# Retention and gated feed-forward on one core: eight instead of ten blocks of the second token group by plain fp32, and transfers spread differently

## The chip, the cores and the metric

The kernel runs on one core of one Trainium2 chip. The metric is the device time of one execution in microseconds (us); lower is better. The median of 3 runs of the kernel before is 608.78 us (608.66 to 608.83). Five engines with queues of their own work side by side: PE multiplies matrices, DVE (VectorE), ACT (ScalarE) and POOL (GpSimd) work on elements, SP only issues transfers (DMAs), which POOL and ACT can issue too.

## The reference, cut to what matters

```python
# q, k, v: (4, 8, 768, 64); gamma: one decay per head
state = gamma * state + outer(k[t], v[t])      # for each batch and head, over 768 steps
y[t]  = scale * (q[t] @ state)
x = y as (3072 tokens, 512)                    # heads side by side
h = x @ w_in                                   # 512 x 2048
out = (h * erf(softplus(h))) @ w_out           # 2048 x 512, all to about fp32 accuracy
```

The weights come as 64-bit floats, so the kernel makes 32-bit ones of them with integer operations on DVE (lines 232 to 280).

## The kernel before, in words

**Units of work.** The sequence is cut into 24 chunks of 128 tokens (6 per batch row); two chunks are a token group of 256, so there are 12 groups, 0 to 11. A "block" (`ft`) is one of the 16 column blocks of 128 of `w_in`.

**Two ways to multiply.** Plain: `hidden_of(ft, g)` (line 691) does one block for one group with four fp32 matmuls of 256 columns; the trace shows each as two records. Split: weights and inputs are split into three fp32r parts, `hi`, `lo` and `dif` (`split_weights` line 315, `split` line 329: ACT makes `hi`, DVE `lo` and `dif`), and three products replace one fp32 product. `unit(g, n)` (line 726) does two blocks for one group: 24 matmuls of 256 columns. `pair_unit(g, ft)` (line 758) does one block for two neighbouring groups: 12 matmuls of 512 columns. In both the eight `hi` and `lo` matmuls of a block come before those that read `dif`.

**Who does which block.** `ALONE` (line 77) says it. Group 0 is done alone by plain matmuls, all 16 blocks. Group 1 is done plainly for its first 10 blocks; blocks 10 to 15 are joined with group 2 in pair units. Blocks 8 and 9 of group 2 are done by one `unit(2, 4)`. From there on each period of eight pair units does eight blocks for two neighbouring groups, up to group 11, whose last blocks are done alone.

**The order is written by hand.** After an opening that works on chunks 0 to 3, the loop at lines 867 to 876 goes through the 16 blocks: plain matmuls for block `ft`, then the steps of `during[ft]` (lines 851 to 866), then `put_hidden`. Steps are chunk work for the retention (`scale_early`, `T`, `begin`, `states`, `results`, `crossed_sums`), conversion of weights (`need`, `convert`, `weight_steps`), splitting, and loads. Then come the periods `g` = 2 to 12 (lines 1081 to 1101): in each, unit `i` runs on PE, `steps(pair, 3)` hands in loads, `load_quarter` hands in quarters of `w_out`, and the steps of that unit follow. `begin` (line 588) is the first PE work of a period's two chunks; it reads `kT` and `qT`, which DVE makes from `kb` and `qb` by a scaling and two transposes (`prepare`, line 553). `results` (line 627) ends them on PE. After the periods `project` (line 964) does the second matrix product.

**Transfers.** SP issues the loads of `w_in` (line 200) and of `kb` and `qb` (line 164: 16 transfers of 32 KB each for a pair of chunks, in pieces of 128 bytes). POOL issues `v` and `kn` of a pair (lines 148 and 158, all four at once), `w_out` (line 213) and all stores of hidden blocks (lines 710, 714, 746, 779, 783). A queue issues in program order, with eight transfers in flight at most: the ninth waits for the first. A hidden block leaves PSUM through an `h` tile of a pool of six (`b2`); the tile is free again when its store has landed. The scales of `qb` lie in `kq_b`: 20 small POOL transfers fetch their beginnings (`load_block_scales`, line 405), DVE does three small operations and POOL five (`block_scales`, line 418).

Of the kernel before, what the change touches and what calls it, by code (L numbers as in the profile page):

```python
# [21 lines left out]
P = 128  # L22
# [10 lines left out]
def head(u, r):  # L33
    return u // 2 + u % 2 * 4 + 2 * r
# [15 lines left out]
def kernel(  # L50
# [23 lines left out]
    DH = d_model // 2  # L74
    FIRST = JPC // 2 - 1

    ALONE = {0: n_ft, 1: 5 * n_ft // 8, NG - 1: n_ft // 2}
    assert D == 64 and d_model == H * D and n_k == HP == 4 and S % GT == 0 and NJ % 2 == 0
    assert H == 8 and n_ft == 16 and NC > JPC and GT == 2 * C

# [11 lines left out]
    def b4(name, shape, dtype=F32):  # L92
        return big.tile([P] + shape, dtype, name=name, tag="b4")
# [50 lines left out]
    def load_values(j, queue=nc.sync):  # L144
        if j % 2 == 0:
            VP[j] = b4("v", [2, H, D])
        V[j] = VP[j - j % 2][:, j % 2]
        queue.dma_start(V[j], of_chunk(v, j))

    def load_pair(j):  # L150

        b, c = divmod(j, NC)
        KNP[j] = b4("kn", [2, H, D])
        KB[j], QB[j] = (b4(name, [HP, 2 * C]) for name in ("kb", "qb"))
        for i in range(2):
            load_values(j + i, nc.gpsimd)
            KN[j + i], SLOT[j + i] = KNP[j][:, i], head
            nc.gpsimd.dma_start(KN[j + i], of_chunk(k, j + i))
        yield
        for to, src in ((KB[j], k), (QB[j], q)):  # L160
            for s, d in itertools.product(range(2), range(2)):
                part = slice((2 * s + d) * 32, (2 * s + d + 1) * 32)
                for u in range(HP):
                    nc.sync.dma_start(
                        to[part, u].rearrange("p (a d) -> p a d", d=32),
                        src[b, head(u, s), c * C : (c + 2) * C, d * 32 : (d + 1) * 32].rearrange(
                            "(a p) d -> p a d", p=32
                        ),
                    )
                yield  # L170

    kq_s = const.tile([P, NC, 2, H], F32, name="kq_s")
# [226 lines left out]
        query_scale(slice(2, NC))  # L399


    kq_b = const.tile([P, 2, HP, NC, 4], F32, name="kq_b")
    by_b = const.tile([P, 2, HP], F32, name="by_b")

    def load_block_scales():
        for s, i in itertools.product(range(2), range(2)):
            nc.gpsimd.dma_start(
                by_b[s * D : (s + 1) * D, 1, 2 * i : 2 * i + 2], decay_s[i * D : (i + 1) * D, s::2]
            )
        for s, d in itertools.product(range(2), range(2)):  # L410
            part = slice((2 * s + d) * 32, (2 * s + d + 1) * 32)
            for u in range(HP):
                nc.gpsimd.dma_start(
                    kq_b[part, 0, u, 0],
                    decay_k[:, head(u, s) : head(u, s) + 1].rearrange("(a p) h -> p (a h)", p=32),
                )

    def block_scales():
        nc.vector.reciprocal(by_b[:, 0], by_b[:, 1])
        nc.vector.reciprocal(kq_b[:, 1, :, 0], kq_b[:, 0, :, 0])  # L420
        nc.vector.tensor_scalar(kq_b[:, 1, :, 0], kq_b[:, 1, :, 0], unscale, None, op0=ALU.mult)
        for c in range(1, NC):
            nc.gpsimd.tensor_tensor(
                kq_b[:, :, :, c], kq_b[:, :, :, c - 1],
                by_b[:, :, :, None].to_broadcast([P, 2, HP, 4]), op=ALU.mult,
            )

    psum_turn = itertools.cycle((ps_r, ps_h))
# [124 lines left out]
    def prepare(j):  # L553


        for name, store, x in (("k", KT, KB[j]), ("q", QT, QB[j])):
            if name == "q":
                own = x.rearrange("p u (a d) -> p u a d", d=32)
                scale = kq_b[:, 1, :, j % NC : j % NC + 2].rearrange("p u c a -> p u (c a)")
# [105 lines left out]
    def crossed_sums(j):  # L665
        g, i = divmod(j, 2)
        for r in range(2):
# [4 lines left out]
            else:  # L672
                nc.vector.tensor_tensor(x, x, SC[j][a][:, 2:, :D], op=ALU.add)

    def split_x(j, n=1):
        g, i = divmod(j, 2)
        if i == 0:
            if not XR:
                XR.extend(
                    ring.tile([P, 3, HP, GT], F32R, name=f"x_{x}", tag=f"x{i}")  # L680
                    for i, x in enumerate(("hi", "lo", "dif"))
                )
            X[g] = [x[:, g % 3] for x in XR]
        at = slice(i * C, (i + n) * C)
        split(X[g], (slice(None), slice(None), at), XC[g][:, :, at])

# [4 lines left out]
    def hidden_of(ft, g):  # L691

        bank, col = (ft, g) if ft < ALONE[1] else (ft - ft % 2, ft % 2)
        if bank not in HP_:
            HP_[bank] = ps_h.tile([P, 2, GT], F32, name="hp")
        w = WF[ft // 2].rearrange("p h a f -> p (h a) f")
        for kk in range(n_k):
            nc.tensor.matmul(  # L698
                HP_[bank][:, col],
                w[:, kk, ft % 2 * P : (ft % 2 + 1) * P], XC[g][:, kk],  # L700
                start=(kk == 0), stop=(kk == n_k - 1),
            )
# [135 lines left out]
    ret_out(JPC - 1, lambda: hidden_of(0, 0), state_last=True)  # L838
    need("in", 1)
    hidden_of(1, 0)  # L840
    A(JPC - 1)


    def steps(s, n=1):
        for _ in range(n):
            next(s, None)

    pair = load_pair(JPC + 2)
    prep, vals = prepare(JPC + 2), values(JPC + 2)
    a, b = JPC, JPC + 1  # L850
    during = {
        1: [(load_block_scales,)],
        2: [(scale_early, a, 1), (steps, pair, 2)],
        3: [(scale_early, a, 0), (T, a, None, ("o2", "o3")), (steps, pair, 2)],
        4: [(scale_early, b, 1), (steps, pair, 2)],
        5: [(scale_early, b, 0), (T, b, None, ("o0", "o1")), (steps, pair, 2)],
        6: [(begin, a, ps_r), (begin, b, None, ("o2", "o3")), (steps, pair)],
        7: [(states, a), (states, b)],
        8: [(results, a, ("o0", "o1")), (results, b), (block_scales,)],
        9: [(crossed_sums, a), (crossed_sums, b), (convert, 2), (split_x, a, 2)],  # L860
        10: [(hi_of, 4), (steps, vals, 1)],
        12: [(split_weights, 4), (hi_of, 5)],
        13: [(split_x, 2, 2), (steps, vals, 1)],
        14: [(split_weights, 5)],
        15: [(steps, prep, 3)],
    }
# [144 lines left out]
        4: (4, 5, 6, 7), 5: (2, 3, 4, 5), 6: (0, 1, 2, 3, 5, 6, 7), 7: (0, 3, 4, 5, 6), 8: (2, 3, 4, 5),  # L1011
    }

    vals = values(2 * JPC)

    def period(g, prep, next_prep):
# [14 lines left out]
        if g < NG:  # L1031
            units = [two(g - 1, ft) for ft in range(8 - 8 * (g % 2), 16 - 8 * (g % 2))]
        if g == G2 + 1:
            return units, joined(3, 5, g), {
                0: [(steps, vals), (hi_of, 2), (steps, prep, 1)],
                1: [(steps, prep, 1), (steps, vals)],
                2: [(split_weights, 2), (hi_of, 3)],
                3: [(states, a), (states, b), (split_weights, 3)],
                5: [(crossed_sums, a), (crossed_sums, b), (split_x, a, 2)],
                7: [(steps, next_prep, 1)],  # L1040
            }, range(4)
        if g < NG - 2:
            return units, joined(2, 5, g), {
                0: [(steps, prep, 4)],
# [34 lines left out]
        }, ()  # L1079

    for g in range(G2, NG + 1):
        pair = load_pair(2 * g + 4) if 2 * g + 4 < NJ else iter(())
# [89 lines left out]
```

## Time and profile before

| what | value |
|---|---|
| median of 3 runs | 608.78 us |
| the profiled execution | 608.73 us, of which the span from first to last instruction is 607.0 us |
| clock granted to PE | full, in every slice |
| busy: PE, DVE, ACT, POOL | 601.5, 462.4, 394.6, 131.4 us |
| plain matmuls (line 698) | 208 records of 256 columns |
| pair units (line 766) | `o` tiles: 296 each of `hi`, `lo`, `dif`; `r` and `hp` tiles: 8 each |
| `unit` (line 732) | `o` tiles: 24 each of `hi`, `lo`, `dif`; `r` and `hp` tiles: 8 each |
| transfers | 109.93 MB in 147692 packets, 103152 of them under 512 bytes |

The page gives each engine's busy time, a strip of 40 slices, the transfer queues, and the chain of work that ended last. "Idle before" is the time in which an engine sat waiting ahead of an instruction. The 1.73 us between the profiled execution's time and its span do not belong to any instruction of the profile. The time of a record is longer than the step from one matmul to the next, since matmuls overlap; below, steps from start to start are used.

### The profile page before, as it was taken

The numbers are of one execution on the slowest core, as the hardware profiler recorded it, in microseconds if no ns is written. First come the engines' busy times: TensorE is split into PE (matmuls) and PEld (weight loads), VectorE is DVE, ScalarE is ACT, GpSimd is POOL, SyncE is SP. The second block draws the span as 40 slices with busy tenths as digits, with TensorE's granted clock in tenths as the row PEclk, the third lists the DMA queues.
The fourth block names the chain that finished last, engine by engine and source line by source line (L and its number), as shares of the span: only waits on it lengthen the run. The fifth ranks groups of instructions, "written<-read, shape, count | busy, mean of one in ns | idle before, by whom it ended". The sixth has DMA issues, their size and how long they took to land.

```text
span 607.0 us, 13097 instructions
## 1 busy us (share of the span) xinstructions
PE 601.5 (99%) x5160; PEld 501.8 (83%) x5160; DVE 462.4 (76%) x579; ACT 394.6 (65%) x620; POOL 131.4 (22%) x223
## 2 busy tenths in 40 slices
PE   8999999999999999999999999999999999999997
PEld 6888888888888888888888988888888888888886
DVE  5899898877978779787778995887777758668540
ACT  3684858354453544435487787899889888988920
POOL 1086463244535535242111200000000000000000
PEclk9999999999999999999999999999999999999999
DMA  9999698988979999795655937145424432531300
GB/s 202 347 260 263 146 245 259 246 180 233 256 194 277 250 261 209 228 233 169 201 163 183 307 122 240 37 140 173 139 72 137 148 104 96 173 125 49 105 35 35
DMA packets 147692, 109.93 MB, mean 181 GB/s; under 512 B 103152, under 2 KB 127472, under 8 KB 147632
## 3 DMA queue, kind: packets, MB, share of 16 engines
q1 hardware_dynamic: 131536, 59.93, 38.7%
q0 software_dynamic: 15536, 49.04, 25.5%
q8 instruction: 40, 0.66, 0.5%
q14 instruction: 20, 0.16, 0.1%
q10 hardware_dynamic: 560, 0.14, 0.1%
HBM read 71.58 MB, written 37.49 MB: 180 GB/s over the span
## 4 chain that ended last, share of the span: by engine, by line
PE 99%; ACT 0%; POOL 0%; issue 0%; DVE 0%; DVEq 0%; POOLq 0%
PE o L766 34%; PE o L981 22%; PE r L981 11%; PE hp L981 11%; PE hp L698 8%; PE o L732 1%; PE hp L594 1%; PE hp L766 1%; PE r L766 1%; PE hp L643 1%; PE r L643 1%; PE r L594 1%; PE r L654 1%; PE r L601 1%; PE o L526 1%; PE r L487 1%
## 5 line engine op out<-in xcount | busy, mean ns | idle before, releaser
L766 PE MATMUL o<-x_hi,w_hi 128*128 128x512 f32 x296 | 117.3, 396 | 0.0
L766 PE MATMUL o<-x_lo,w_lo 128*128 128x512 f32 x296 | 115.3, 390 | 0.0
L340 ACT ACTIVATE h<-o 128x512 f32<-128x512 f32 x70 | 41.5, 594 | 90.6 <-PE o L766 87.9
L936 DVE TENSOR_TENSOR e<-hid,e 128x1024 f32<-128x1024 f32 x48 | 56.6, 1221 | 53.2 <-ACT e L926 53.2
L766 PE MATMUL o<-x_dif,w_dif 128*128 128x512 f32 x296 | 79.1, 389 | 0.0
L341 DVE SCALAR_TENSOR_TENSOR h<-o,h 128x512 f32<-128x512 f32 x70 | 47.8, 686 | 30.0 <-ACT h L340 25.6
L783 POOL DMA_DIRECT2D hids<-h x72 | 40.4, 562 | 137.3 <-DVE h L341 136.8
L766 PEld LDWEIGHTS o<-x_hi,w_hi 128*128 128x128 f32 x296 | 55.5, 188 | 12.3
L766 PEld LDWEIGHTS o<-x_dif,w_dif 128*128 128x128 f32 x296 | 55.6, 188 | 11.5
L766 PEld LDWEIGHTS o<-x_lo,w_lo 128*128 128x128 f32 x296 | 55.6, 188 | 11.0
L334 DVE SCALAR_TENSOR_TENSOR g_dif<-g_hi,g_lo 128x1024 fp32r<-128x1024 f32 x48 | 58.8, 1225 | 3.6 <-DVE g_lo L333 0.5
L332 ACT ACTIVATE g_hi<-e 128x1024 fp32r<-128x1024 f32 x48 | 51.0, 1062 | 15.3 <-DVE e L936 12.7
L333 DVE TENSOR_TENSOR g_lo<-e,g_hi 128x1024 fp32r<-128x1024 f32 x48 | 58.6, 1221 | 0.1
L922 ACT ACTIVATE e<-hid 128x1024 f32<-128x1024 f32 x48 | 48.3, 1053 | 0.8 <-DVE hid L917 0.6
L926 ACT ACTIVATE e<-e 128x1024 f32<-128x1024 f32 x48 | 48.2, 1052 | 0.3
L981 PE MATMUL o<-w_hi,g_hi 128*128 128x512 f32 x120 | 46.7, 389 | 0.0
L981 PE MATMUL o<-w_lo,g_lo 128*128 128x512 f32 x120 | 46.7, 389 | 0.0
L981 PE MATMUL o<-w_dif,g_dif 128*128 128x512 f32 x120 | 46.7, 389 | 0.0
L698 PE MATMUL hp<-xT,w 128*128 128x256 f32 x208 | 46.3, 381 | 0.0
L698 PEld LDWEIGHTS hp<-xT,w 128*128 128x128 f32 x208 | 39.0, 190 | 5.3
L578 ACT ACTIVATE v<-v,kq_s 128x64 f32<-128x64 f32 x144 | 35.6, 335 | 0.0
L922 ACT ACT_TABLE_LOAD x24 | 30.8, 1283 | 4.2 <-DVE hid L917 2.9
(211 smaller groups left out, 1249.0 us busy)
## 6 DMA issues: line engine op xcount, KB each, us to landing
hids<-h POOLq DMA_DIRECT2D x72, 256.0 KB, 4.0
hid<-hids SPq DMA_DIRECT2D x36, 512.0 KB, 4.9
raw<-in_moe_w_in_dram SPq DMA_DIRECT2D x32, 256.0 KB, 5.5
raw<-in_moe_w_out_dram POOLq DMA_DIRECT2D x32, 256.0 KB, 6.3
out_dram<-y SPq DMA_DIRECT2D x23, 256.0 KB, 2.1
kb<-in_k_dram SPq DMA_DIRECT2D x144, 32.0 KB, 3.9
v<-in_v_dram POOLq DMA_DIRECT2D x18, 256.0 KB, 6.2
kn<-in_k_dram POOLq DMA_DIRECT2D x18, 256.0 KB, 7.1
```

The lines of the kernel that those rows point to most:

```text
L332: nc.scalar.activation(hi, x, AF.Copy, scale=KEEP)
L333: nc.vector.tensor_tensor(lo, x, hi.bitcast(F32), op=ALU.subtract)
L334: nc.vector.scalar_tensor_tensor(dif, hi.bitcast(F32), Z, lo.bitcast(F32), op0=ALU.mult, op1=ALU.subtract)
L340: nc.scalar.activation(to, a, AF.Copy, scale=1 + 1 / Z)
L341: nc.vector.scalar_tensor_tensor(to, b, -1 / Z, to, op0=ALU.mult, op1=ALU.add)
L698: nc.tensor.matmul(HP_[bank][:, col], w[:, kk, ft % 2 * P : (ft % 2 + 1) * P], XC[g][:, kk], start=(kk == 0), stop=(kk == n_k - 1),)
L766: nc.tensor.matmul(to, W[n][i][:, kk * 2 * P + u * P : kk * 2 * P + (u + 1) * P], XR[i][:, at, kk], start=(kk == 0 and i == parts[0]), sto ...
L783: nc.gpsimd.dma_start(HID2[g][:, ft % 8], h)
L922: nc.scalar.activation(E[n], HID_[n], AF.Softplus)
L926: nc.scalar.activation(E[n], E[n], AF.Erf)
L936: nc.vector.tensor_tensor(E[n], HID_.pop(n), E[n], op=ALU.mult)
L981: nc.tensor.matmul(Y[g][t][x // 2], G[n][x][:, f, t * P : (t + 1) * P], W_OUT[ft // 2][x][:, ft % 2 * d_model : (ft % 2 + 1) * d_model], s ...
```

## The change

It has five parts.

1. `ALONE[1]` goes from 10 to 8. Group 1 is plain for blocks 0 to 7; blocks 8 to 15 are eight pair units with group 2. `unit(2, 4)` is gone. The period `g = 2` has eight units and no longer seven.
2. Steps are reordered. Two weight steps go ahead of the last state addition of the opening. In `during`, conversions go ahead of `results` and `crossed_sums` at blocks 8 and 9, and the split of the inputs is cut into `hi_x`, `lo_x`, `last_x`: at block 12 DVE does both `lo` of the inputs, then `lo` and `dif` of weight 4, then both `dif` of the inputs.
3. `v` and `kn` of a pair (`load_natural`) are handed in one chunk at a time, at units 0, 1, 3 and 4.
4. For the pair of chunks 6 and 7, eight of the sixteen `qb` transfers go to POOL; the other eight and all `kb` stay on SP.
5. The quarters of `w_out` are handed in at units 4 to 7, no longer 0 to 3, in the periods `g = 2` and `g = 3`. The beginnings of `kq_b` are copied on chip from `kq_s` by 16 transfers, after two small POOL copies; the three DVE operations go, and `kq_b` holds only the half for `q`.

```diff
-    ALONE = {0: n_ft, 1: 5 * n_ft // 8, NG - 1: n_ft // 2}
+    ALONE = {0: n_ft, 1: n_ft // 2, NG - 1: n_ft // 2}
...
-    def load_pair(j):
+    def load_natural(j):
...
         for i in range(2):
             load_values(j + i, nc.gpsimd)
+            yield
+        KNP[j] = b4("kn", [2, H, D])
+        for i in range(2):
             KN[j + i], SLOT[j + i] = KNP[j][:, i], head
             nc.gpsimd.dma_start(KN[j + i], of_chunk(k, j + i))
-        yield
...
+        for n, (s, d) in enumerate(parts):
+            blocks(KB[j], k, s, d, nc.sync)
+            if n > 1 and j < 2 * JPC:
+                blocks(QB[j], q, 1, n - 2, nc.gpsimd)
+            yield
+        for n, (s, d) in enumerate(parts):
+            if n < 2 or j >= 2 * JPC:
+                blocks(QB[j], q, s, d, nc.sync)
                 yield
...
     def load_block_scales():
...
+        for s, d, a in itertools.product(range(2), range(2), range(4)):
             nc.gpsimd.dma_start(
+                kq_b[(2 * s + d) * 32 : (2 * s + d + 1) * 32, :, 0, a],
+                first_b[a * 32 : (a + 1) * 32, s],
+            )
...
     def block_scales():
-        nc.vector.reciprocal(by_b[:, 0], by_b[:, 1])
-        nc.vector.reciprocal(kq_b[:, 1, :, 0], kq_b[:, 0, :, 0])
-        nc.vector.tensor_scalar(kq_b[:, 1, :, 0], kq_b[:, 1, :, 0], unscale, None, op0=ALU.mult)
...
+    def hi_x(g):
+        place_x(g)
+        nc.scalar.activation(X[g][0], XC[g], AF.Copy, scale=KEEP)
+
+    def lo_x(g):
+        hi, lo, dif = X[g]
+        nc.vector.tensor_tensor(lo, XC[g], hi.bitcast(F32), op=ALU.subtract)
+
+    def last_x(g):
+        hi, lo, dif = X[g]
+        nc.vector.scalar_tensor_tensor(
+            dif, hi.bitcast(F32), Z, lo.bitcast(F32), op0=ALU.mult, op1=ALU.subtract
+        )
...
     hidden_of(1, 0)
+    next(weight_steps)
+    next(weight_steps)
     A(JPC - 1)
...
-        8: [(results, a, ("o0", "o1")), (results, b), (block_scales,)],
-        9: [(crossed_sums, a), (crossed_sums, b), (convert, 2), (split_x, a, 2)],
-        10: [(hi_of, 4), (steps, vals, 1)],
-        12: [(split_weights, 4), (hi_of, 5)],
-        13: [(split_x, 2, 2), (steps, vals, 1)],
+        8: [(convert, 2), (results, a, ("o0", "o1")), (results, b), (block_scales,)],
+        9: [(convert, 1), (crossed_sums, a), (crossed_sums, b), (hi_x, JPC // 2)],
+        11: [(hi_of, 4), (hi_x, 1)],
+        12: [(lo_x, JPC // 2), (lo_x, 1), (split_weights, 4), (last_x, JPC // 2), (last_x, 1), (steps, vals, 1)],
+        13: [(hi_of, 5), (steps, vals, 1)],
...
-            units = [one(g, 4)] + [two(1, ft) for ft in range(ALONE[1], n_ft)]
+            units = [two(1, ft) for ft in range(ALONE[1], n_ft)]
...
-            }, range(4)
+            }, range(4, 8)
...
-            steps(pair, 3)
+            steps(natural, NATURAL.count(i))
+            steps(pair, 2 if i == 0 else 3)
```

More of the change, by code (lines that the diff above doesn't have):

```diff
@@ L148, in load_values, with blocks @@
         queue.dma_start(V[j], of_chunk(v, j))
+    def load_natural(j):
+        for i in range(2):
+            load_values(j + i, nc.gpsimd)
+            yield
+        KNP[j] = b4("kn", [2, H, D])
+        for i in range(2):
+            KN[j + i], SLOT[j + i] = KNP[j][:, i], head
+            nc.gpsimd.dma_start(KN[j + i], of_chunk(k, j + i))
+            yield
     def load_pair(j):
         b, c = divmod(j, NC)
-        KNP[j] = b4("kn", [2, H, D])
         KB[j], QB[j] = (b4(name, [HP, 2 * C]) for name in ("kb", "qb"))
[L155 to L158, printed above, removed]
-        yield
[L160 to L169, printed above, removed]
+        def blocks(to, src, s, d, queue):
+            part = slice((2 * s + d) * 32, (2 * s + d + 1) * 32)
+            for u in range(HP):
+                queue.dma_start(
+                    to[part, u].rearrange("p (a d) -> p a d", d=32),
+                    src[b, head(u, s), c * C : (c + 2) * C, d * 32 : (d + 1) * 32].rearrange(
+                        "(a p) d -> p a d", p=32
+                    ),
+                )
+        parts = list(itertools.product(range(2), range(2)))
+        for n, (s, d) in enumerate(parts):
+            blocks(KB[j], k, s, d, nc.sync)
+            if n > 1 and j < 2 * JPC:
+                blocks(QB[j], q, 1, n - 2, nc.gpsimd)
+            yield
+        for n, (s, d) in enumerate(parts):
+            if n < 2 or j >= 2 * JPC:
+                blocks(QB[j], q, s, d, nc.sync)
                 yield
@@ L399, in other_scales @@
         query_scale(slice(2, NC))
-    kq_b = const.tile([P, 2, HP, NC, 4], F32, name="kq_b")
-    by_b = const.tile([P, 2, HP], F32, name="by_b")
+    kq_b = const.tile([P, HP, NC, 4], F32, name="kq_b")
+    by_b = const.tile([P, HP], F32, name="by_b")
+    first_b = const.tile([P, 2, HP], F32, name="first_b")
     def load_block_scales():
-        for s, i in itertools.product(range(2), range(2)):
+        for s in range(2):
+            nc.gpsimd.tensor_copy(
+                first_b[:, s].rearrange("p (c i) -> p c i", c=2),
+                kq_s[:, 0, 1].rearrange("p (i s c) -> p s c i", i=2, s=2)[:, s],
+            )
+        for s, d, a in itertools.product(range(2), range(2), range(4)):
             nc.gpsimd.dma_start(
-                by_b[s * D : (s + 1) * D, 1, 2 * i : 2 * i + 2], decay_s[i * D : (i + 1) * D, s::2]
-            )
[L410 to L416, printed above, removed]
-    def block_scales():
-        nc.vector.reciprocal(by_b[:, 0], by_b[:, 1])
-        nc.vector.reciprocal(kq_b[:, 1, :, 0], kq_b[:, 0, :, 0])
-        nc.vector.tensor_scalar(kq_b[:, 1, :, 0], kq_b[:, 1, :, 0], unscale, None, op0=ALU.mult)
+                kq_b[(2 * s + d) * 32 : (2 * s + d + 1) * 32, :, 0, a],
+                first_b[a * 32 : (a + 1) * 32, s],
+            )
+    def block_scales():
+        for s in range(2):
+            own = slice(s * D, (s + 1) * D)
+            nc.gpsimd.tensor_copy(
+                by_b[own].rearrange("p (c i) -> p c i", c=2),
+                d_s[own].rearrange("p c (i s) -> p s c i", s=2)[:, s],
+            )
         for c in range(1, NC):
             nc.gpsimd.tensor_tensor(
-                kq_b[:, :, :, c], kq_b[:, :, :, c - 1],
-                by_b[:, :, :, None].to_broadcast([P, 2, HP, 4]), op=ALU.mult,
+                kq_b[:, :, c], kq_b[:, :, c - 1], by_b[:, :, None].to_broadcast([P, HP, 4]), op=ALU.mult
             )
@@ L558, in prepare @@
                 own = x.rearrange("p u (a d) -> p u a d", d=32)
-                scale = kq_b[:, 1, :, j % NC : j % NC + 2].rearrange("p u c a -> p u (c a)")
+                scale = kq_b[:, :, j % NC : j % NC + 2].rearrange("p u c a -> p u (c a)")
                 nc.vector.tensor_tensor(
@@ L673, in crossed_sums, with place_x @@
                 nc.vector.tensor_tensor(x, x, SC[j][a][:, 2:, :D], op=ALU.add)
+    def place_x(g):
+        if not XR:
+            XR.extend(
+                ring.tile([P, 3, HP, GT], F32R, name=f"x_{x}", tag=f"x{i}")
+                for i, x in enumerate(("hi", "lo", "dif"))
+            )
+        X[g] = [x[:, g % 3] for x in XR]
+    def hi_x(g):
[8 more added lines that the diff above has]
+            dif, hi.bitcast(F32), Z, lo.bitcast(F32), op0=ALU.mult, op1=ALU.subtract
+        )
     def split_x(j, n=1):
@@ L677, in split_x @@
         if i == 0:
[L678 to L683, printed above, removed]
+            place_x(g)
         at = slice(i * C, (i + n) * C)
@@ L846, in steps @@
             next(s, None)
-    pair = load_pair(JPC + 2)
+    natural, pair = load_natural(JPC + 2), load_pair(JPC + 2)
     prep, vals = prepare(JPC + 2), values(JPC + 2)
@@ L852 @@
         1: [(load_block_scales,)],
-        2: [(scale_early, a, 1), (steps, pair, 2)],
+        2: [(scale_early, a, 1), (steps, natural, 4), (steps, pair, 1)],
         3: [(scale_early, a, 0), (T, a, None, ("o2", "o3")), (steps, pair, 2)],
@@ L1012 @@
     }
+    NATURAL = (0, 1, 3, 4)
     vals = values(2 * JPC)
@@ L1040, in period @@
                 7: [(steps, next_prep, 1)],
-            }, range(4)
+            }, range(4, 8)
         if g < NG - 2:
@@ L1081 @@
     for g in range(G2, NG + 1):
+        natural = load_natural(2 * g + 4) if 2 * g + 4 < NJ else iter(())
         pair = load_pair(2 * g + 4) if 2 * g + 4 < NJ else iter(())
```

## The prediction

> **What bounds the kernel now.** I read the page's busy times and its chain first, then the chain in order of time, then the rows of DVE in the stretch where the change sits, then the transfers by stretch.
>
> ```profile
> PE 601.5 (99%) x5160; PEld 501.8 (83%) x5160; DVE 462.4 (76%) x579; ACT 394.6 (65%) x620; POOL 131.4 (22%) x223
> ...
> PE 99%; ACT 0%; POOL 0%; issue 0%; DVE 0%; DVEq 0%; POOLq 0%
> ```
>
> PE is the bound and hardly waits: of the span's 607.0 us it is busy for 601.5, and the rest lies in the first 20 us and behind the last matmul (PE ends at 603.4). In the table of stretches PE is busy for 5.00 of every 5 us from 20 to 100 us. So the change can only give what it takes out of PE's own list, and can only lose where something new makes PE wait.
>
> ```profile
> 39.28 6.91 PE hp L698 x32
> ...
> 52.53 7.11 PE hp L698 x32
> 61.66 14.01 PE hp L698 x64
> 75.67 2.87 PE o L732 x24
> 78.54 5.47 PE o L766 x24
> 86.03 5.67 PE o L766 x24
> 93.52 13.82 PE o L766 x60
> ```
>
> The chain in order of time (start, us, what): plain matmuls, then the one unit (2, 4) of 24 matmuls, then pair units of 12, with retention work in the gaps. This is where the change works.
>
> **PE's sum, from start to start.** Taken out:
> - Two plain blocks of group 1, 16 records. From the rows 61.59 to 75.32 us, 64 records take 13.73, so 0.2145 each; from 26.05 to 38.24, 56 take 12.19, so 0.2177. Sixteen are 3.43 to 3.48; I take 3.46.
> - Unit (2, 4). With the pair units behind it, PE goes from 75.32 (first split matmul) to 83.94 (first matmul of `begin`): 8.62 for the unit and two pair units.
>
> Put in: three pair units stand there. A pair unit inside a row of them takes 2.72 (99.02 to 101.74), one ahead of retention work 2.81 (81.13 to 83.94), one behind it 2.85 (85.97 to 88.82). The first one behind plain matmuls is not in the trace: the unit's first matmul cost 0.19 extra there (0.31 for 0.12), which gives 2.91 at most, and 2.75 (first behind the unit) at least; I take 2.87. So 2.87 + 2.72 + 2.81 = 8.40 for 8.62, and one more pair unit follows `results`: 2.72. Sum: -3.46 - 8.62 + 8.40 + 2.72 = **-0.96**, with bounds -1.10 and -0.87. The order of instructions shows that the change does this: eight plain matmuls and 24 of line 732 less, 24 of the pair unit more.
>
> So 608.73 - 0.96 = 607.77 in terms of the profiled execution, which lies 0.05 below the median 608.78; I write 607.8.
>
> **What must now come earlier: DVE.** PE reaches the first split matmul at 75.32 - 3.46 = 71.86. It then needs `lo` of weight 4 and of both inputs at once (72.1), and all three `dif` 1.84 later (78.38 to 80.22 in a pair unit): 73.7.
>
> ```profile
> 26.17 0.42 DVE L547 TENSOR_TENSOR state<-state,o 128x256 f32<-128x256 f32 x1 [1.21 <-PE o L534]
> ...
> 55.31 0.17 DVE L419 RECIPROCAL by_b<-by_b 128x4 f32<-128x4 f32 x1
> ...
> 61.46 0.49 DVE L673 TENSOR_TENSOR xT<-xT,o 128x128 f32<-128x128 f32 x2 [1.04 <-ACT xT L662]
> 62.39 0.48 DVE L673 TENSOR_TENSOR xT<-xT,r 128x128 f32<-128x128 f32 x2 [0.45 <-ACT xT L662]
> ...
> 66.10 1.22 DVE L333 TENSOR_TENSOR x_lo<-xT,x_hi 128x1024 fp32r<-128x1024 f32 x1 [0.41 <-ACT x_hi L332]
> ...
> 74.55 1.23 DVE L334 SCALAR_TENSOR_TENSOR x_dif<-x_hi,x_lo 128x1024 fp32r<-128x1024 f32 x1
> 75.69 1.22 DVE L325 SCALAR_TENSOR_TENSOR w_lo<-w_hi,w 128x1024 fp32r<-128x1024 f32 x1
> ```
>
> These are DVE's rows, with its waits in brackets. Between 26 and 75.69, when the last `dif` of the inputs ends, it waits in these four places only: it is DVE that has no room here. The reordering fills them. The two weight steps ahead of the state addition (0.42, 0.42, 0.69, 0.42 long) fill the 1.21. The three scale operations go (55.31 to 55.74: 0.43). Conversions placed ahead of `crossed_sums` cover some of 1.04 + 0.45 + 0.41 = 1.90. The same work then ends between 75.69 - 1.21 - 0.43 - 1.90 = 72.15 and, with none of the 1.90 filled, 74.05. I take 72.2, since by the rows ACT's copies of `results`, 1.75 earlier than before, stand ready when DVE comes: 1.5 us to spare, cost nothing. All `lo` end three operations of 1.2 earlier.
>
> Edits that cost nothing, with their cover:
> - The state addition of the opening comes 0.6 later (26.75), its ACT copy ends at 27.6, and PE reads it at 27.8, behind `hidden_of(1, 0)`. The weight piece that the moved steps read was issued by 18.7 and lands 4.3 to 6.4 later, by 25.1 at the latest. If the cover fails, some 0.1 to 0.3.
> - `begin` moves to 71.86 + 8.40 = 80.3. DVE needs 2.4 for weight 5 and 3.6 for `kT`, the scaling and `qT`: 72.2 + 6.0 = 78.2.
> - In every later period more room is left, not less: three pair units, no longer two, stand between `results` of `g = 2` and the first use of its input. Where chunk 10's `qb` came late (the only DVE wait for a transfer at `prepare`, 1.35 us; `qT` ended at 130.03 for a `begin` at 130.84), SP, with eight of its sixteen `qb` transfers gone (half of the 9.64 that they took), is now about 4.8 us ahead. Next to be late there is ACT's scaling of `v`, which ended at 129.0.
> - `v` and `kn` one at a time: four POOL issues of 0.9, nobody waits; they are read a period later.
> - The second product's group 1 reads one more `low` tile: one DVE addition of 0.69 near 354 us. The parts of that block are done at 359 and read at 385.8.
>
> **Transfers.**
>
> ```profile
> core 0: us, PE busy (x) PEld busy (x) DVE busy (x) ACT busy (x) POOL busy (x), PEclk, DMA share, GB/s
> 50.00:55.00 5.00, 5.00 (x127) 4.32 (x126) 4.93 (x10) 1.86 (x3) 3.04 (x7) 1.00 1.14 258
> 55.00:60.00 5.00, 5.00 (x50) 4.18 (x52) 4.90 (x10) 0.58 (x1) 1.71 (x4) 1.00 1.07 289
> 65.00:70.00 5.00, 5.00 (x25) 4.41 (x24) 4.52 (x6) 5.00 (x14) 1.23 (x3) 1.00 0.71 171
> ```
>
> The last two columns are the share of the DMA engines in use and the rate. Eight `qb` transfers move from SP at 62 to 71 us, where the share is 0.6 to 0.7, to POOL at 48 to 57, where it is over 1. On POOL they stand ahead of the stores of blocks 3 and 4, so those leave up to 3 us later: eight issues of about 0.55, less the fewer and earlier scale transfers (POOL reaches line 714 at 45.02 now, some 2.5 earlier then), plus waits for a free place among eight in flight. I put the store of block 3 at 54 and its landing at 58.5 (4.3 for 128 KB); its `h` tile is next written at 65. Slack 6.5 us.
>
> [...]
>
> **The rivals.**
> - *DVE comes late to the first pair unit.* The gaps are not filled, because ACT or the transfers set them: then `dif` is ready at 74.05 (only the 1.90 stays) to 75.26 (the 1.21 too), PE waits 0.35 to 1.56, and the time is 608.1 to 609.3. For it: DVE is 4.9 of 5 us busy from 30 to 60. Against it: the weights of that stretch were in place without one DVE wait for a transfer. Chance 0.16.
> - *The queues come late, and the kernel is slower.* Place: `begin` of `g = 2`, which needs `qb` whole on both queues. SP's slowest rows for such transfers are 12 in 12.92 and 16 in 19.17, 1.2 each: then SP ends at 48.42 + 20 x 1.2 = 72.4, and with a landing of 5.4 the data are there at 77.8; 2.5 of scaling and transpose end at 80.3, just in time. From there each us later is one of PE. It decides at 81.0: a stall of 3.2 gives 610.0, and one of 5 611.8. For it: the transfers go into the fullest stretch. Against it: 32 KB blocks took 3.1 to 5.3 to land there, so I expect them by 71. Chance 0.10.
> - *More is gained than the sum.* The pair units run closer than 2.72, or PE's first 20 us change: 607.3. Nothing in the rows shows room for it. Chance 0.05.
> - *The sum is right*: 607.6 to 607.9, 0.69.
>
> **How the numbers follow.** 608.78 less 0.2% is 607.56, plus 0.2% is 610.0; about so much a measurement of this kernel can tell from no change. The forecast lies within, near its lower edge; a twentieth of it falls beyond, which with the third rival makes 0.10 faster. Within: 0.64 and the first rival's 0.16, 0.80. Slower: 0.10. The range takes in the bounds of the sum and the first rival: 607.4 to 609.4.
>
> **What would show it.** Right: 192 plain records, no line 732 on `o` ahead of the periods of pair units but 304 pair-unit records each of `hi`, `lo`, `dif` there; the first split matmul at 71.9 without a PE gap, `begin` at 80.3, and from then on the same distances, all 0.9 to 1.0 earlier. DVE's 1.21 gone, its last `dif` done by 73.7. Wrong: a PE gap at 71.9, 73.7 or 80.3, with DVE or a transfer named as releaser; ACT's `h` waiting for a store; or a DVE wait for `raw` near 25.

## The result and the profile after

The changed kernel takes **610.42 us** (median of 10 runs, 609.59 to 611.83) where the kernel before takes 608.65 (10 runs, 608.21 to 608.98). The ratio is 1.0032, 95% interval 1.0022 to 1.0041: slower, by some 1.8 us, where 0.96 less was forecast, and outside the range of 607.4 to 609.4. The profiled execution took 610.86 us, its span 609.1. Note the spread: 2.2 us, three times that of the kernel before.

The page's busy times, the instruction queue (transfers, MB, share of the DMA engines) and the chain's shares:

```profile
PE 600.6 (99%) x5144; PEld 499.8 (82%) x5144; DVE 461.9 (76%) x577; ACT 395.5 (65%) x621; POOL 140.0 (23%) x228
...
q8 instruction: 40, 0.66, 0.5%
...
PE 96%; SPq 2%; DMA 1%; issue 1%; ACT 0%; DVE 0%; DVEq 0%
```

PE works 0.9 us less, as forecast, and the span is 2.1 longer. In the chain "issue" has gone from 0 to 1%: time in which PE waited for nothing that the profile shows. (SPq and DMA in that line are the first 18 us, where the chain now runs over the first loads; PE's first plain matmul is at 21.75, before at 22.04.)

Where the change was made, all is as expected. The chain in order of time, then DVE's rows:

```profile
69.83 2.16 PE hp L734 x10
71.98 8.20 PE o L802 x36
80.19 0.62 PE hp L613 x32
```

```profile
64.54 2.35 DVE L708 TENSOR_TENSOR x_lo<-xT,x_hi 128x1024 fp32r<-128x1024 f32 x2
...
69.22 2.39 DVE L712 SCALAR_TENSOR_TENSOR x_dif<-x_hi,x_lo 128x1024 fp32r<-128x1024 f32 x2
```

Three pair units run without a gap; both `dif` of the inputs end at 71.61, two us before PE needs them. At the `begin` of `g = 3` PE is 1.09 us ahead of the kernel before (106.18 for 107.27) and stays so for 75 us. The loss comes later, in a period that the change does not touch. Here is `begin` of `g = 8` and what follows it, before and after:

```profile
262.49 0.47 PE hp L601 x32
262.95 0.47 PE r L594 x32
263.42 0.47 PE r L601 x32
263.89 8.39 PE o L766 x36
```

```profile
261.88 0.47 PE hp L620 x32
262.34 0.47 PE r L613 x32
262.81 0.46 PE r L620 x30
263.27 2.02 issue
265.30 0.27 PE r L620 x2
265.57 8.41 PE o L802 x36
```

PE stops two matmuls ahead of the end of a group of 32 like ones that wait for nothing new. The waits of PE say the same (line, releaser, us, times, longest):

```profile
PE r L620 <- issue: 2.0, 1, 2.0
```

**The account**, from start to start, in us: opening -0.29 (it varies by that much from run to run); matmuls -0.79; a stop at 185.39, +0.40; the stop at 263.05, +2.30; all that is left between the first split matmul and the last one, +0.08; the end behind PE's last matmul 4.03 for 3.59, +0.44. Sum +2.14, and 610.86 - 608.73 = 2.13.

**A first theory.** The instruction queue in the page moved 0.66 MB in 40 transfers, 16 KB each, for the 10,374 records that PE and its sequencer left (matmuls, weight loads and semaphore steps): 259 to a transfer. Counted in order of time from 0, PE's first record behind the stop at 185.39 is number 4545 and behind that at 263.05 number 6593: 2048 apart, eight times 256. In both places a transfer of that queue had landed 1.36 and 1.43 us before PE went on. So the theory is that PE had run out of instructions: it had used up one block, and the next was late. `begin` is a run of 256 small matmuls and weight loads that pass in 2.1 us; 256 instructions of pair units take 29. In the changed kernel one block holds just this `begin`. It has 31 instructions less ahead of it than the kernel before (16 matmuls, 16 weight loads, one more semaphore step), where the block holds 33 instructions of the pair unit in front as well (some 3.8 us) and `begin` up to its last 33. The transfers at that time are no denser than before: the share in use from 260 to 265 us is 1.00 in both (last two columns: share, GB/s; before, then after).

```profile
260.00:265.00 5.00, 5.00 (x142) 4.17 (x141) 4.50 (x10) 2.20 (x3) 4.24 (x6) 1.00 1.00 180
```

```profile
260.00:265.00 5.00, 3.27 (x132) 2.66 (x131) 4.92 (x9) 1.75 (x2) 2.99 (x4) 1.00 1.00 196
```

The rival: the transfers of parts 3 to 5 delay the blocks, wherever they begin.

### The profile page after: what moved, and what is told of

Its sections match the earlier page's. It is cut to its first block, busy times and chain, and to the rows that moved or that the text cites. A ratio compares the mean times of both kernels' runs of the same rounds, so it can differ in the third digit from the quotient of the medians.

```text
span 609.1 us, 13061 instructions
## 1 busy us (share of the span) xinstructions
PE 600.6 (99%) x5144; PEld 499.8 (82%) x5144; DVE 461.9 (76%) x577; ACT 395.5 (65%) x621; POOL 140.0 (23%) x228
## 4 chain that ended last, share of the span: by engine, by line
PE 96%; SPq 2%; DMA 1%; issue 1%; ACT 0%; DVE 0%; DVEq 0%
PE o L802 35%; PE o L1019 21%; PE r L1019 11%; PE hp L1019 11%; PE hp L734 7%; PE o L768 1%; PE hp L613 1%; DMA kq<-in_k_dram 1%; PE hp L802 1%; PE r L802 1%; SPq L141 1%; PE hp L662 1%; PE r L662 1%; PE r L620 1%; PE r L613 1%; PE r L673 1%
## 5 line engine op out<-in xcount | busy, mean ns | idle before, releaser
L802 PE MATMUL o<-x_hi,w_hi 128*128 128x512 f32 x304 | 120.8, 397 | 0.1
L802 PE MATMUL o<-x_lo,w_lo 128*128 128x512 f32 x304 | 118.5, 390 | 0.0
L802 PE MATMUL o<-x_dif,w_dif 128*128 128x512 f32 x304 | 81.2, 389 | 0.0
L802 PEld LDWEIGHTS o<-x_hi,w_hi 128*128 128x128 f32 x304 | 57.0, 188 | 13.2 <-issue 0.6
L802 PEld LDWEIGHTS o<-x_dif,w_dif 128*128 128x128 f32 x304 | 57.1, 188 | 11.9
L802 PEld LDWEIGHTS o<-x_lo,w_lo 128*128 128x128 f32 x304 | 57.1, 188 | 11.3
L734 PE MATMUL hp<-xT,w 128*128 128x256 f32 x192 | 42.8, 381 | 0.0
L734 PEld LDWEIGHTS hp<-xT,w 128*128 128x128 f32 x192 | 35.9, 190 | 5.0
```

The source lines that it names most:

```text
L734: nc.tensor.matmul(HP_[bank][:, col], w[:, kk, ft % 2 * P : (ft % 2 + 1) * P], XC[g][:, kk], start=(kk == 0), stop=(kk == n_k - 1),)
L802: nc.tensor.matmul(to, W[n][i][:, kk * 2 * P + u * P : kk * 2 * P + (u + 1) * P], XR[i][:, at, kk], start=(kk == 0 and i == parts[0]), sto ...
```

## The experiments

Times are medians, with the range of the runs; a stop is a step between two of PE's records of over 0.35 us behind 22 us that no semaphore and no fall of the granted clock explains. "Border n" is record 193 + 256 n, counted from 0. The expectations look at the 296 instructions ahead of a border: behind 400 us, where PE's steps are even, a block's transfer (the n-th of the queue for border n) begins in all twenty profiles with PE 266 to 298 records ahead of the border. The kernel before, run beside each batch of experiments, took 608.59 to 608.85.

### Shift the instructions, or move the transfers (e1 to e4)

e1 and e2 change PE's list alone:

```diff
-    keep_warm(7)
+    keep_warm(6)          # e2: keep_warm(2)
+    for _ in range(8):    # e2: 56
+        nc.tensor.matmul(idle[:64, 0, :16], ident[:64, :64], ident[:64, :16], start=True, stop=True)
```

> The changed kernel, and ahead of everything on PE eight tiny fp32 matmuls (64 rows, 16 columns, into the warm-up tile that nobody reads) in place of one of the seven warm-up blocks: 32 more PE instructions, in time that PE spends waiting for the first data. Theory A, the border of an instruction block: the trace has 40 transfers of 16 KB on an instruction queue for 10,374 records of PE, so 256 instructions each; PE's two stops of the changed kernel (2.24 us within `begin` at 263.05, 0.40 at 185.39) stand at its records 6593 and 4545, which are 8 x 256 apart, each right behind a run of some 256 small matmuls and weight loads of `begin`, and each ends 1.4 us after such a transfer has landed. The change takes 31 instructions out of PE's list ahead of the periods; 32 put back move the borders to where they stood before. A expects no stop of PE behind 22 us and 608.0 to 608.4 (608.7 less 0.8 of matmuls, plus 0.4 for the longer end behind the last matmul). Rival B, the transfers: what parts 3 to 5 spread differently delays the instruction blocks, wherever they begin; then the stops stay and the time is 610.0 to 611.0.

Measured: 610.85 us (608.55 to 611.11), the profiled run 609.54, and in it **no stop at a border**. What holds it up there is another thing, in the opening: DVE waits 1.28 us for a raw piece, and the state addition behind it (line 568 here) lets PE wait from 27.3 on, a step of 1.47. Without that the run would have taken 608.3. But the median lies in the range of rival B and above that of theory A, so only the profile speaks for the theory here; what holds up the other runs was not seen.

```profile
25.86 0.43 DVE L252 TENSOR_SCALAR power<-raw 128x512 uint32<-128x512 uint32 x1 [1.28 <-DMA raw<-in_moe_w_in_dram]
...
27.61 0.41 DVE L568 TENSOR_TENSOR state<-state,o 128x256 f32<-128x256 f32 x1
```

> The kernel before, with 56 such tiny matmuls at the start in place of five of the seven warm-up blocks: 224 instructions more, so that the borders (every 256) stand where they stand with 32 fewer, as in the changed kernel. Theory A expects PE to stop at the end of `begin` of g = 8 and, less, of g = 5, by 1 to 2.7 us in all, and 609.5 to 611.5, though no transfer and no period is changed; the opening may cost up to 1 us by itself, which the trace tells. Rival B expects no stop and 608.6 to 609.6.

Measured: 622.90 us (621.86 to 623.99). The opening took 10.8 us longer, not 1, so the time says nothing. By the records there are 220 instructions more and not 224, since one large warm-up matmul went as well. But PE, which has no stop in the kernel before, now stops at 121.14, 129.41 and 278.06, by steps of 2.12, 1.10 and 1.22, at borders 10, 11 and 26. The last lies right behind `begin` of `g = 8`, which was named; the others were not.

e3 is part 1 alone in the kernel before (`1: n_ft // 2` in `ALONE`, and no `one(g, 4)`):

> The kernel before with part 1 alone: eight plain blocks of group 1 and no unit (2, 4), the old order of the steps and the old transfers. By the prediction's first rival PE waits at the first pair units, since `dif` of group 1 ends at 75.3 where it is needed at 73.7: 0.3 to 1.6 us; the matmuls give back 0.8. Theory A adds the stops at the block borders, since 31 instructions are gone here too: 0.4 to 2.7 us, so 609.0 to 612.0. Rival B (transfers) expects no stop at `begin` behind 100 us and 608.2 to 609.4.

Measured: 614.03 us (613.18 to 616.09), above the range; stops at 58.24, 110.38, 118.21 and 266.45 (steps of 1.33, 1.17, 0.92, 1.15), all at borders (4, 9, 10, 25), with the transfers of the kernel before. At 72.83 PE waits for DVE's `lo` besides: the first three pair units take 9.09 us, in the changed kernel 8.49.

e4 is parts 3 to 5 alone (`ALONE[1]` of 10, `one(g, 4)`, the old order of steps):

> The kernel before with parts 3 to 5 alone (transfers handed in differently, scales copied on chip, `qb` on POOL; ten plain blocks and the old order; with seven units in `g = 2` the quarters of `w_out` go to units 3 to 6 there, 4 to 7 in `g = 3`). PE's list is that of the kernel before. Theory A expects no stop and 608.6 to 609.1, the upper end with 0.4 more behind the last matmul. Rival B expects the stops of the changed kernel: 610.3 to 611.5.

Measured: 608.70 us (608.56 to 608.94), ratio 1.0000 (0.9991 to 1.0008), no stop. The rival falls: the transfers of the change alone bring no stop, and old transfers with the short list bring four.

### Four shifts of one kernel (e5 to e8)

The base has the two weight steps behind the state addition again. The shift is made as in e1, but with the tiny matmuls in two corners of the array in turn.

```diff
     hidden_of(1, 0)
-    next(weight_steps)
-    next(weight_steps)
     A(JPC - 1)
```

> The changed kernel with the two weight steps behind the last state addition of the opening again, all else as changed. In e1 PE waited 1.2 us at 27.3 because DVE's state addition stood behind weight steps whose raw piece had landed at 25.8 only. If that is one of the two causes (theory: the block borders and the raw piece), the stops at the block borders stay, the wait in the opening goes in every run: 609.0 to 611.0, lower than the changed kernel by some 0.5 in the median. If the wait in the opening was a thing of e1 alone, the time is that of the changed kernel, 610.4, with the same spread of 2 us.

Measured: 612.06 us (610.12 to 614.15). Stops at 115.31, 185.67 and 264.99 (0.37, 2.05, 2.00): borders 10, 17 and 25, the last two those of the changed kernel. The time lies above what was expected in either case. So the place of the weight steps is not what slows the changed kernel.

> e5 with 32 more PE instructions at the start (eight tiny matmuls in place of one warm-up block), so that the block borders stand as in the kernel before. If both causes are right and there is no third: no stop of PE of over 0.3 us behind 22 us, 607.9 to 608.5, and a spread of under 1 us. If the borders do not matter: as e5.

Measured: 609.68 us (608.05 to 610.46), no stop. The opening of the profiled run (609.68) is 1.6 us longer than e5's; without that, 608.0. The median and the spread of 2.4 us miss what the theory expected.

> e5 with 104 more PE instructions (26 tiny matmuls in place of three warm-up blocks): by the trace's records the places where the 296 instructions ahead of a border pass in under 7.2 us are one in place of five. Theory A: no stop or one small one (near 58), 607.9 to 608.6. If the borders do not matter: as e5.

Measured: 610.62 us (609.92 to 611.55), no stop; the opening 2.6 us longer, without it the profiled 610.61 would be 608.1. The median misses the range of the theory, with an opening that it had left out.

> e5 with 168 more PE instructions (42 tiny matmuls in place of three warm-up blocks; the opening may take up to 2 us longer, which the trace tells): now five borders, the 7th, 11th, 15th, 19th and 27th block, lie right behind a run of small matmuls (296 instructions in 6.2 to 6.8 us). Theory A: stops at two or more of these borders, and nowhere else, 1 to 5 us in all: 609.5 to 614, beside what the opening takes. If the borders do not matter: as e5, beside the opening.

Measured: 616.10 us (615.45 to 617.48), the opening 4.3 us longer. Stops at 87.26, 164.20 and 242.01 (0.94, 0.66, 1.69): borders 7, 15 and 23. Two were named and 23 was not (its 296 instructions take 6.8 us in the same list; I had left it out); 11, 19 and 27 did not stop. The last, in the chain:

```profile
241.30 0.47 PE r L619 x32
241.77 0.46 PE r L626 x31
242.23 1.48 issue
243.71 0.27 PE r L626
```

The same picture as in the changed kernel, one matmul ahead of the end of `begin`, one period earlier: the stop moves with the count. (By the records e7 and e8 have 100 and 164 instructions more than e5, four fewer than was expected.)

What the longer openings are: PE comes to its full pace later. The score matmuls at 8 to 10 us in e6 follow each other by 0.21 us, in the changed kernel by 0.105. The trace's first record of PE's granted clock, at full, begins at 10.00 us in e6 and at 5.78 in the changed kernel; ahead of its first record a trace says nothing of the clock, though the views print full there (so for the kernel before the clock is shown from 7.12 us on, not in every slice). In the twelve profiles with an opening of 21.5 to 22.1 us this first record begins at 4.33 to 7.65, in the eight with a longer one at 10.00 to 19.93.

### Another way to shift, and the end (e9 to e12)

The warm-up's 11 blocks of 128 columns, in three places, are made as 22 matmuls of 64 columns, 88 PE instructions for 16:

```diff
-        for i in range(0, n, 4):
-            m = min(4, n - i)
-            nc.tensor.matmul(idle[:, :m], ident, ident[:, None, :].to_broadcast([P, m, P]), start=True, stop=True)
+        for i in range(2 * n):
+            nc.tensor.matmul(idle[:, 0, :D], ident, ident[:, :D], start=True, stop=True)
```

> [...] Of the borders only four, 4, 5, 7 and 10, keep less than 7.6 us for the 296 instructions ahead of them. If the block borders and the raw piece are the whole cause: no stop or small ones, first plain matmul at 21.5 to 22.1, and 608.0 in the runs in which the raw piece lands in time, up to 2 more in the others. If something else costs time: 609.5 and more in all runs.

> e9 with the two weight steps behind the state addition again, as in e5. The theory: 608.0 (607.8 to 608.4) and the spread of the kernel before, under 1 us, since neither the borders nor the raw piece can hold PE. If the moved steps cost nothing: as e9, in median and spread.

> e9 with one store of the output, the first of the 24, issued by POOL and no longer by SP. The end behind PE's last matmul took 3.6 us where SP issues 437 or 429 transfers and 4.03 where it issues 430 or 438: SP waits for its eight semaphores one after the other, 0.06 each, and with 430 that of the last store comes third, so that five more waits follow it. 429 transfers here: the end takes 3.6 again, 0.4 less than e9 in every run: 607.6. If the end has another cause: as e9.

> The kernel before with parts 1 and 2 alone, and the warm-up of e9; the transfers and scales as before. PE's list is that of e9. If parts 3 to 5 do nothing for PE: as e9, 608.0 to 609. By the prediction's row of chunk 10 (`qT` ended 0.73 ahead of `begin` in the kernel before, behind a wait for `qb`) PE would now be there 0.8 to 1.1 earlier and wait 0.1 to 0.4 at `begin` of `g = 4` near 129.8.

Measured: 611.40, 612.73, 612.48 and 615.08 us. None of the four times can be compared with the others: the narrow warm-up made the opening 2.8, 3.1, 3.0 and 5.2 us longer than in the kernel before. Three things can be read from their traces. e9 and e12 have no stop; e10 and e11 have one each, 1.23 at 297, at border 29, which was not among the four that were named for e9. e11's end behind the last matmul is 3.61 us, e9's 4.01: the **end** is settled. In e9 the third of SP's last waits is over at 608.16 and seven more follow, 0.06 apart; in e11 eight are over by 608.34 and the long ones come last. In all twenty profiles it is 3.6 with 437 or 429 transfers on SP and 4.0 with 430 or 438. And in e12 PE waits nowhere at the `begin` of `g = 4`: the expected 0.1 to 0.4 did not come (DVE had no wait for `qb` there).

### A shift that leaves the opening alone (e13 to e16)

The plain matmuls of some blocks of group 0 are cut in two, 16 instructions more for a block:

```diff
+        parts = 2 if g == 0 and ft < 8 else 1     # e14: 2, e15: 6
-        for kk in range(n_k):
+        for i in range(parts):
+            for kk in range(n_k):
+                at = slice(i * GT // parts, (i + 1) * GT // parts)
...
-                HP_[bank][:, col],
+                    HP_[bank][:, col, at],
```

> The kernel before, in which the plain matmuls of group 0's blocks 0 to 7 are made as two of 128 columns each instead of one of 256: 128 more PE instructions by the time of the first pair unit, the same products, the opening as it was. The cost of the cut itself is at most 1.6 us (32 matmuls by 0.01 to 0.05). By the records, four borders (15, 19, 23, 27) then lie behind `begin` with 6.2 to 6.5 us for 296 instructions. Theory of the borders: PE stops at two or more of the borders 7, 8, 10, 11, 15, 19, 23, 27 and nowhere else, 1 to 4 us in all: 610 to 614, with a spread of over 1 us. If position plays no part: 608.8 to 610.4 without stops.

Measured: 611.25 us (609.80 to 611.51), ratio 1.0038 (1.0025 to 1.0051). First plain matmul 21.77, so the opening is as it was. Stops at 61.41 (0.76, border 5, not named) and 239.26 (0.91, border 23, named):

```profile
238.75 0.47 PE r L601 x32
239.22 0.43 PE o L769
239.65 0.52 issue
240.17 5.87 PE o L769 x25
```

> As e13 with blocks 0 and 1 alone: 32 more instructions, which leave only border 29 with less than 7.5 us. Theory of the borders: no stop but perhaps 1 us at 293; 608.8 to 609.2 (0.1 to 0.4 for the cut). If the cut itself were what stops PE: a quarter of e13's loss.

Measured: 610.34 us (608.92 to 611.01), ratio 1.0024 (1.0014 to 1.0034): 1.1 above the range that was expected. One stop, 0.95 at 294.94, at border 29 as named; 0.8 more of this profiled run lies outside the span, which no row explains. So the kernel before becomes about as slow as the changed one by a cut that takes 0.12 us by its rows (first plain to first split matmul 53.40 for 53.28).

> The changed kernel with the weight steps behind the state addition (e5), the first output store on POOL (e11) and the cut of e13 for six blocks: 96 more instructions, one border (5, near 61) left with 6.5 us. Theory: no stop behind 70 us; 608.7 less 0.7 of matmuls plus 0.3 to 1.2 for the cut: 608.2 to 609.2. If other things hold the changed kernel up: 609.5 and more.

Measured: **608.15 us** (607.58 to 608.56), ratio 0.9991 (0.9982 to 1.0000), no stop. From the first plain to the first split matmul it takes 0.30 more than the changed kernel (the cut). 608.73 - 0.79 + 0.30 + 0.04 of opening = 608.28, and the profiled run is 608.27. So the changed kernel's matmuls are worth the 0.79 of the account above, once the borders and the end are out of the way.

```profile
PE 600.6 (99%) x5192; PEld 502.0 (83%) x5192; DVE 461.6 (76%) x577; ACT 395.8 (65%) x621; POOL 139.7 (23%) x229
```

> The changed kernel with the weight steps behind the state addition, the first output store on POOL and the eight tiny matmuls of e1 (32 instructions; e1's opening was not longer). Borders 13, 29 and 21 lie as in the kernel before. Theory: no stop, 607.4 to 608.0 in most runs, faster than the kernel before by 0.7 to 1.2. If the openings or stops of e1 come back: 609 and more.

Measured: 609.87 us (607.98 to 610.19), ratio 1.0012 (1.0004 to 1.0021). The profiled run, 608.20, has no stop and is 0.2 above the range that was expected; eight of the eleven are above 609. What holds those up was not seen. Its first clock record begins at 5.02; that PE came to its pace later in the others is possible and not shown.

### The new order of steps (e17, e18)

> e15 with the two weight steps ahead of the state addition, as in the changed kernel: the only difference. If their place costs time where the raw piece lands late (e1: 1.2 us): a spread of over 1 us and a median of 608.5 to 610. If it costs nothing: e15's 608.15 and its spread of 1 us.

Measured: 608.22 us (607.96 to 608.78), ratio 0.9994 (0.9985 to 1.0002): as e15. The place of the two steps costs nothing and gives nothing here.

This run is also the cleanest test of the borders. It is the changed kernel but for the 96 instructions of the cut and the one store, and its median is 2.2 us lower (608.22 for 610.42), its range 0.8 us wide for 2.2. The end gives 0.4 of it and the cut takes 0.3, so 2.1 go to the shift. The cut by itself gives nothing: in the kernel before it cost 2.7 (e13) and 1.8 us (e14).

> e15 with the order of steps at blocks 8 to 13 as in the kernel before, so that nothing of part 2 is left. In e15 DVE ends the last `dif` of the inputs at 72.7 for a first split matmul at 72.26 that needs it 1.8 later. By the prediction's step the old order leaves DVE's waits of up to 1.90 unfilled and puts `lo` of the second input behind the weights: PE should wait at its first pair unit for DVE, by 0.4 to 1.6 us, and the time is 608.5 to 609.8. If ACT or the transfers, not the order, set DVE's pace: as e15.

Measured: 608.86 us (608.58 to 609.09), ratio 1.0004 (0.9995 to 1.0013), 0.7 above e15. PE's first pair unit waits for DVE's `lo` of the second input, which stands behind the weights (DVE's row, then PE's wait):

```profile
71.66 1.22 DVE L350 TENSOR_TENSOR x_lo<-xT,x_hi 128x1024 fp32r<-128x1024 f32 x1
```

```profile
PE o L805 <- DVE x_lo L350: 0.3, 1, 0.3
```

The wait is counted from PE's modelled ends; from start to start the first three pair units take 8.99 us, in e15 8.49: 0.5.

### All stops

| kernel | borders with a stop (step, us) | from landing to going on, us |
|---|---|---|
| changed | 17 (0.52), 25 (2.24) | 1.36, 1.43 |
| e2 | 10 (2.12), 11 (1.10), 26 (1.22) | 1.56, 1.49, 1.46 |
| e3 | 4 (1.33), 9 (1.17), 10 (0.92), 25 (1.15) | 1.55, 1.54, 1.39, 1.52 |
| e5 | 10 (0.37), 17 (2.05), 25 (2.00) | 1.35, 1.58, 1.52 |
| e8 | 7 (0.94), 15 (0.66), 23 (1.69) | 1.44, 1.63, 1.37 |
| e10, e11 | 29 (1.23), 29 (1.23) | 1.53, 1.56 |
| e13, e14 | 5 (0.76), 23 (0.91); 29 (0.95) | 1.49, 1.53; 1.32 |
| before, e1, e4, e6, e7, e9, e12, e15 to e18 | none | |

There are twenty stops. All are at the first record of a block, all ended 1.3 to 1.6 us after its transfer had landed, and all lie in or right behind `begin` or `results`. The other side agrees: the twenty profiles have 791 borders, and at none of them did PE go on sooner than 1.30 us after that landing. The number of transfers fits too: 40 in every run that ends ahead of border 40, 41 in every run that passes it.

At the other 771 of the 791 borders PE crosses without a stop; at the twenty stops the measured step is 0.37 to 2.24 us.

What is not settled is why a block's transfer starts when it does. It began when PE stood between 7 and 298 records ahead of the border, mostly over 100. Where the 256 records ahead of a border pass in under 2.5 us, fifteen times in the twenty profiles, the start divides them: in seven cases the transfer had begun before PE came to the border before, and there is no stop; in eight it had not, and all eight have a stop. In the kernel before, for example, the 256 records ahead of border 21 pass in 1.89 us, the transfer having begun 3.2 us before PE came there; in the changed kernel that of border 25 began 0.6 before. That other transfers stand in its way is the author's estimate from the share in use around the stop at 263.05 (1.00 from 260 to 265 us); no run took them away.

## Why the prediction was wrong

**The step that failed** is the first: that the change "can only lose where something new makes PE wait", with the waits looked for among the kernel's own engines and transfers. The sum took instructions out of PE's list as time alone. It also moved every later instruction 31 places against the borders of 256, and that cost 2.7 us in the profiled run. The views that would have shown it were there: 40 transfers on an instruction queue, runs of 256 small matmuls, and the records to count.

Point by point:

- *PE's sum, -0.96 (-1.10 to -0.87; by its own terms the upper bound is -0.89).* Measured -0.79, a little outside. The sixteen plain records gave 3.40 for 3.46. The three pair units in a row took 8.49 for 8.40 (the first, behind plain matmuls, about 2.95 for 2.87); the one more behind `results` 2.74 for 2.72. e15 confirms the size.
- *DVE must come earlier.* Right: last `dif` at 71.61 (72.2 forecast), no wait at 71.9, 73.7 or 80.3. The first rival's mechanism is real with the old order: 0.5 us by e18's rows, 0.7 by its median, within its 0.35 to 1.56. It is the order at blocks 8 to 13 that does it, not the two steps ahead of the state addition (e17).
- *Edits at no cost.* Parts 3 to 5 cost nothing (e4). The raw piece that was to land "by 25.1 at the latest" kept DVE until 25.86 in e1, and the price of that, put at 0.1 to 0.3, was 1.2 there; it was not seen again. `qT` of chunk 10 is ready at 127.58 for a `begin` at 129.75.
- *Transfers.* The eight `qb` issues on POOL took 0.58 to 0.61 us each, against the 0.55 that was taken for one, with DVE 4.67 to 4.93 of 5 us busy beside them.
- *The slower rival* had the sign and not the mechanism: `qT` of the first pair is done at 77.56 for a `begin` at 80.12. Its sum is off too: with 607.8 as its base, stalls of 3.2 and 5 give 611.0 and 612.8, not 610.0 and 611.8.
- *The end behind the last matmul* was taken as fixed. It is 0.44 longer, because SP's transfers went from 437 to 430.

That the shift costs the median some 2 us is shown by e17; how far each of the ten runs was held up at which border is argued from one profile: without its stops it would have taken 608.1, and the fastest of the ten, 609.59, is 1.5 above that. Open are also the longer runs of e1, e6 and e16, whose profiles have no stop at a border, and e14's time outside the span.

## What to carry to other kernels

Where an engine is the bound and its list has runs of many very short instructions, count the instructions, not only their time: here 31 instructions fewer shifted all later block borders, 256 records apart, and the sign to look for was the spread between runs, 2.2 us for 0.8. To tell such a loss from the edit's own worth, compare at several shifts (here a few matmuls cut in two), and read the edit's gain from start to start within a stage. The gain here, 0.79 us of 608, was smaller than what the shift of the instruction stream cost (some 2 us by e17), and the number of transfers on SP cost 0.44 more.

## What the runs showed of the hardware

- A stop can have a sequel. Behind e5's stop at 264.99 the granted clock fell to half for 3.4 us (third column from the right, 0.71 over four us), and seven matmul steps took 0.43 us and one 0.37, for 0.23; in the changed kernel's profile a stop as long had no such sequel, nor had the other eighteen.

```profile
266.00:270.00 4.00, 3.01 (x10) 2.33 (x10) 0.89 (x2) 0.00 (x0) 0.00 (x0) 0.71 0.93 298
```

- e2's 56 tiny matmuls at the start took 12.1 us (0.11 for each of 112 records), where the seven large warm-up blocks at the start of the kernel before take 3.33; and e2's first record of the full clock begins at 19.93 us, that of the kernel before at 7.12. Behind them the score matmuls still follow each other by 0.21 us (18.02 to 19.30), from 21.86 on by 0.10 to 0.11: 12 us of back-to-back matmuls of 64 rows and 16 columns had not brought PE to its full pace.
- The end of this kernel depends on the number of SP's transfers: with 437 or 429 (both leave 5 when divided by its eight semaphores) it takes 3.6 us, with 430 or 438 (both leave 6) 4.0. Other remainders were not run.
